# Block sums of the gated tokens on VectorE instead of GpSimd, next tokens' steps at every second unit, and the last product by output half

## The chip, the cores and the metric

The kernel runs on one core of a Trainium2 chip. The metric is the time of one execution on the device, in microseconds (us).

## The reference

Three layers follow each other: attention with keys and values averaged in groups of 8, a layer of products `(a * b @ w3) @ w_out`, and a layer with a gate. The change touches the last alone:

```python
def _moe2_ref(x, w_in, w_out):        # x: 4608 x 512, w_in: 512 x 2048, w_out: 2048 x 512
    h = x @ w_in
    g = h * (1.0 / (1.0 + np.exp(-1.702 * h)))
    return (g @ w_out).astype(np.float32)
```

## The kernel before

Tokens are taken in 9 blocks of 512. Every factor of a product is kept as two parts, a rounded one ("hi", made by a cast on ScalarE) and its residue ("lo", a subtraction on VectorE); each product is three matmuls of 128x512 (`mm3u`, L709). The last layer handles block 0 plainly and the other eight in four passes of two blocks (`for pr`, L911), in which each pair of 2x2 block products is done with seven products instead of eight (M1 to M7), as in Strassen's scheme: the factors are sums and differences of blocks.

A pass has two parts. The **gate part** runs over four groups `fp` of the hidden dimension. In each, PE does the products of `ORDER` (84 matmuls, and in the first three groups 12 more, "O", for the output); ScalarE and VectorE bring them from PSUM into the tiles g11, g12, g22 and g21 and apply the gate (`gelu`, L858). At the end of a group three block sums are formed (L987, GpSimd): g11 = g12 - g11, t2 = g22 - g11 and g12 = g22 - g12. They are factors of the output products.

The **output part** (from L1022) has six products (`OUT`: M2, M6, M5, M7, M4, M3) of four units each, 24 units of 12 matmuls; the first unit is followed by 12 more for M1. After each unit `make` prepares one more moving tile (`mv`, four buffers): a cast (L104) on ScalarE and a residue (L105) on VectorE from one of the block sums. Beside it each unit takes one step of `late` (the results of the product before: add L1017, transpose L730, four stores L736) or, where there is none, one of `prep`. `prep` is the twelve steps of `x_prep` for the next pass's tokens: the load of four tiles (L784, SP), eight differences (L792, each with a cast and a residue, tiles sx and xM), and three splits (L109, L110). A fourth block sum per group, g21 = g21 - t2 (L1004, GpSimd), follows four of the `make` steps.

Weights stream through six slots (`pull`, L702, tiles st) on SP's queue. In pass 1 there are also the 32 steps `wsum` on weights (L826, L831, L832, L834), a few of them in each group.

The order of instructions on each engine is not the code's order: a planner lays them out when the program is built, by their order in the code and by when it takes them to be ready. On the chip each engine runs its list in that order.

Of the kernel before, what the change touches and what calls it, by code (L numbers as in the profile page):

```python
# [12 lines left out]
ALU = mybir.AluOpType  # L13
# [4 lines left out]
P = 128  # L18
T = 512
# [3 lines left out]
def pooled_attention_moe_moe2(  # L23
# [648 lines left out]
    with tc.tile_pool(name="pb", bufs=1, reuse_waits="tile") as pb, \  # L672
# [7 lines left out]
        def freed(*bs):  # L680
            for i, _ in bs:
                banks.append(i)
# [43 lines left out]
        def out_tile():  # L726
            return pb.tile([P, T // 32, 2, 32], F32, name="ot", tag="ot")
# [129 lines left out]
        def gelu(o, i):  # L857
            nc.scalar.activation(o, i, AF.Gelu_apprx_sigmoid)  # L858
# [52 lines left out]
        for pr in range(1, NPAIR + 1):  # L911
            X = xc.pop(pr)
            bA = []
            G = []
            mvs = {}

            def out_mm(bs, name, fp, first, last):
                g, w = mvs.pop((name, fp)), ready.pop(("o", pr, name, fp))
                for m in range(2):
                    for i in range(2):  # L920
                        mm3u(bs[m][1], w[:, i], m, g[:, :, i], first and i == 0, last and i == 1)
                pull()

            for fp in range(NFP):
                g11, g12, g22, g21, t2 = (gtile(a * NFP + fp) for a in range(5))
                G.append((g11, g12, g22, g21, t2))
                C, Z, W = [None] * 2, [None] * 2, [None] * 2
                m1, U, V = [None] * 2, [None] * 2, [None] * 2
                for name, i in ORDER:
                    if name == "O":  # L930
                        if fp < NFP - 1:
                            if fp == 0:
                                bA += [bank() for _ in range(2)]
                            out_mm(bA, "M1", fp, fp == 0, False)
                        continue
                    if name in PART:
                        s, h = PART[name]
                        w = ready[s, pr, 2 * fp + i][:, h]
                    else:
                        w = ready[name, pr, fp][:, i]  # L940
                    bs = W if name == "M2" else Z if name in ("M5", "M3") else C
                    first = name in ("M1", "M2", "M5")
                    if first:
                        bs[i] = bank()
                    o = bs[i][1]
                    for j in range(2):
                        mm3u(o, w, j, X[name][:, :, j], first and j == 0, j == 1)
                    if name == "M1":
                        m1[i] = tmp("m")
                        nc.scalar.copy(m1[i], o)  # L950
                    elif name == "M2":
                        ready.pop(("a", pr, 2 * fp + i))
                        pull()
                        nc.vector.tensor_tensor(out=g11[:, i], in0=o, in1=m1[i], op=ALU.add)
                        freed(W[i])
                        if i:
                            gelu(g11, g11)
                            g = mvs["M1", fp] = moving()
                            split(g, g11, nc.vector)
                    elif name == "M6":  # L960
                        U[i] = tmp("u")
                        nc.scalar.copy(U[i], o)  # L962
                    elif name == "M5":
                        ready.pop(("s", pr, 2 * fp + i))
                        pull()
                    elif name == "M7":
                        V[i] = tmp("m")
                        nc.scalar.copy(V[i], o)
                        nc.vector.tensor_tensor(out=g22[:, i], in0=Z[i][1], in1=V[i], op=ALU.add)
                        if i:  # L970
                            gelu(g22, g22)
                    elif name == "M4":
                        gelu(g21[:, i], o)
                        freed(C[i])
                    elif name == "M3":
                        nc.vector.tensor_tensor(out=g12[:, i], in0=o, in1=U[i], op=ALU.add)
                        freed(Z[i])
                        if i:
                            gelu(g12, g12)
                    if i and name in ("M7", "M4", "M3"):  # L980
                        ready.pop((name, pr, fp))
                        pull()
                    if wsum and (name, i) in (("M2", 1), ("M5", 0), ("M7", 0), ("M4", 0),
                                              ("M6", 1), ("M7", 1), ("M4", 1)):
                        wsum.pop(0)()
                for o, p, m in ((g11, g12, g11), (t2, g22, g11), (g12, g22, g12)):
                    nc.gpsimd.tensor_tensor(out=o, in0=p, in1=m, op=ALU.subtract)  # L987
            while wsum:
                wsum.pop(0)()


            prep = x_prep(pr + 1) if pr < NPAIR else []
            src = {"M5": 0, "M7": 1, "M3": 2, "M2": 3, "M4": 3, "M6": 4}
            todo_mv = [(name, fp) for name, _ in OUT for fp in range(NFP)]
            t4 = list(range(NFP))

            def make():
                if todo_mv:
                    name, fp = todo_mv.pop(0)
                    g = mvs[name, fp] = moving()  # L1000
                    split(g, G[fp][src[name]], nc.vector)
                    if t4 and (name, fp) in (("M6", 0), ("M6", 2), ("M5", 0), ("M5", 2)):
                        t = G[t4.pop(0)]
                        nc.gpsimd.tensor_tensor(out=t[3], in0=t[3], in1=t[4], op=ALU.subtract)  # L1004

            m1, U, V, n = [], [], [], 0
            b0, b1 = 2 * pr - 1, 2 * pr
            late = []

            def out_of(name, bs):  # L1010
                ot = out_tile()
                add, blk, i = {"M2": (m1, b0, 0), "M7": (V, b1, 1),
                               "M4": (None, b0, 1), "M3": (U, b1, 0)}[name]

                def part(m):
                    if add:
                        nc.vector.tensor_tensor(out=add[m], in0=bs[m][1], in1=add[m], op=ALU.add)  # L1017
                    turn_out(ot, m, add[m] if add else bs[m][1])

                def end():  # L1020
                    part(1)
                    store(ot, blk, i)  # L1022

                return [lambda: part(0), end]

            make()
            make()
            for name, u in OUT:
                if name == "M2":
                    bW = [bank() for _ in range(2)]  # L1030
                elif name == "M5":
                    bZ = [bank() for _ in range(2)]
                bs = bW if name == "M2" else bZ if name in ("M5", "M3") else bA
                for fp in range(NFP):
                    out_mm(bs, name, fp, name in ("M2", "M5") and fp == 0, fp == NFP - 1)
                    make()
                    if name == "M2" and fp == 0:
                        out_mm(bA, "M1", NFP - 1, False, True)
                        for m in range(2):
                            m1.append(tmp("m"))  # L1040
                            nc.scalar.copy(m1[m], bA[m][1])
                        make()
                    if late:
                        late.pop(0)()
                    elif prep:
                        prep.pop(0)()
                    n += 1
                if name == "M6":
                    for m in range(2):
                        U.append(tmp("u"))  # L1050
                        nc.scalar.copy(U[m], bA[m][1])
                elif name == "M7":
                    for m in range(2):
                        V.append(tmp("m"))
                        nc.scalar.copy(V[m], bA[m][1])
                if name in ("M2", "M7", "M4", "M3"):
                    late += out_of(name, bZ if name == "M7" else bs)
                if name == "M2":
                    freed(*bW)
                elif name == "M4":  # L1060
                    freed(*bA)
            while late:
                late.pop(0)()
            freed(*bZ)
            while prep:
                prep.pop(0)()

# [29 lines left out]
```

## Time and profile before

| | us |
|---|---|
| three runs | 1496.11, 1495.22, 1498.04 (median 1496.11) |
| the profiled run | 1496.16 |
| span of the profiled run, first to last instruction | 1494.0 |
| busy in that span: PE | 1441.0 |
| VectorE (DVE) | 962.9 |
| ScalarE (ACT) | 693.8 |
| GpSimd (POOL) | 662.1 |

The four passes run from 856 us to the end. Times in the rows below are microseconds from the span's start, durations in microseconds unless marked ns. PE is the matmuls, SPq and ACTq are the queues that issue transfers. A row of a timeline may hold several instructions of one kind, with their count; in brackets stands how long the engine was idle before it and what ended that. Matmuls are pipelined: one has a record of 0.39 us, and the next begins before it ends.

### The profile page before, as it was taken

To read this page: it belongs to the slowest core of one execution; us is meant where nothing else is said; L and a number is where in the kernel's file an instruction comes from. 1 tells how busy PE (TensorE), PEld (TensorE's weight loads), DVE (VectorE), ACT (ScalarE), POOL (GpSimd) and SP (SyncE) were. 2 spreads that over 40 slices of the span, in tenths; PEclk is the share of its full clock that TensorE was granted. 3 is DMA by queue.
4 is the path that set the end of the run, shared out by engine and by line. 5 is a ranking of instruction groups with operands and counts; after the bars stand their busy time and mean duration, and the time that the engine had idled before them with its cause. 6 is when DMAs were issued, how large, how long until landed. Compare 5 with 4: busy or idle time off the path is not lost.

```text
span 1494.0 us, 19448 instructions
## 1 busy us (share of the span) xinstructions
PE 1441.0 (96%) x6536; PEld 1189.5 (80%) x6536; DVE 962.9 (64%) x1664; ACT 693.8 (46%) x1212; POOL 662.1 (44%) x653
## 2 busy tenths in 40 slices
PE   4988999999999999999999998999999999999998
PEld 3766888888888888888888876778877888788886
DVE  7888998878787877555627255583339433853354
ACT  6974444434343433365635344442455244534442
POOL 7787856555555555366833122500532043302530
PEclk9989999999999999999999999999999999999999
DMA  9991342323232311199879887767676866786665
GB/s 276 242 226 34 65 89 52 77 49 77 48 77 48 76 33 37 61 321 350 307 248 385 285 271 269 272 184 230 198 231 214 230 195 213 230 235 187 200 208 138
DMA packets 292323, 267.64 MB, mean 179 GB/s; under 512 B 199552, under 2 KB 224128, under 8 KB 292224
## 3 DMA queue, kind: packets, MB, share of 16 engines
q1 hardware_dynamic: 291648, 265.35, 59.0%
q10 hardware_dynamic: 576, 1.05, 0.2%
q8 instruction: 52, 0.85, 0.2%
q14 instruction: 47, 0.39, 0.1%
HBM read 209.72 MB, written 56.62 MB: 178 GB/s over the span
## 4 chain that ended last, share of the span: by engine, by line
PE 83%; DVE 6%; DMA 5%; ACT 2%; issue 2%; POOL 2%; SPq 0%; DVEq 0%; POOLq 0%; ACTq 0%
PE bk L709 38%; PE wk L114 8%; PE wk L116 8%; PE wk L115 8%; PE acc L114 5%; PE acc L116 4%; PE acc L115 4%; PE wk L278 2%; DMA xM<-x2d 2%; PE bk L115 1%; PE bk L116 1%; PE bk L114 1%; POOL cv L172 1%; DVE p L314 1%; DMA st<-wud 1%
## 5 line engine op out<-in xcount | busy, mean ns | idle before, releaser
L709 PE MATMUL bk<-mv,st 128*128 128x512 f32 x1104 | 263.6, 394 | 9.6 <-DVE mv L105 4.6
L709 PE MATMUL bk<-xM,st 128*128 128x512 f32 x1140 | 268.4, 390 | 1.9 <-ACT u L962 1.9
L709 PEld LDWEIGHTS bk<-mv,st 128*128 128x128 f32 x1104 | 209.2, 190 | 56.3 <-DVE mv L105 5.9
L709 PEld LDWEIGHTS bk<-xM,st 128*128 128x128 f32 x1140 | 214.4, 188 | 46.9 <-ACT u L962 2.3
L114 PE MATMUL wk<-s,s 128*128 128x512 f32 x576 | 228.1, 398 | 6.5 <-DVE a L641 3.8
L987 POOL TENSOR_TENSOR s<-g,s 128x1024 f32<-128x1024 f32 x16 | 38.8, 2423 | 426.0 <-ACT g L858 426.0
L115 PE MATMUL wk<-s,s 128*128 128x512 f32 x576 | 225.5, 392 | 0.1
L116 PE MATMUL wk<-s,s 128*128 128x512 f32 x576 | 225.3, 392 | 0.1
L314 DVE STREAM_TRANSPOSE p<-s_t 32x160 f32<-32x160 f32 (+1 forms) x560 | 178.5, 319 | 10.5
L105 POOL TENSOR_TENSOR s<-a,s 128x512 fp32r<-128x512 f32 x56 | 73.4, 1310 | 155.0 <-ACT s L104 121.2
L116 PE MATMUL acc<-s,s 128*128 128x512 f32 x352 | 139.4, 396 | 1.8 <-DVE s L105 1.8
L105 DVE TENSOR_TENSOR mv<-g,mv 128x1024 fp32r<-128x1024 f32 x80 | 112.9, 1411 | 43.8 <-ACT mv L104 42.6
L115 PE MATMUL acc<-s,s 128*128 128x512 f32 x352 | 139.5, 396 | 1.2 <-POOL s L105 1.1
L114 PE MATMUL acc<-s,s 128*128 128x512 f32 x352 | 131.9, 400 | 7.6 <-DVE s L105 4.5
L114 PEld LDWEIGHTS wk<-s,s 128*128 128x128 f32 x576 | 108.9, 189 | 30.8 <-DVE a L641 5.0
L116 PEld LDWEIGHTS wk<-s,s 128*128 128x128 f32 x576 | 108.7, 189 | 23.3 <-DVE s L105 0.5
L115 PEld LDWEIGHTS wk<-s,s 128*128 128x128 f32 x576 | 108.6, 189 | 22.2 <-DVE s L391 0.5
L172 POOL TENSOR_TENSOR cv<-cv,s 128x512 int32<-128x512 int32 x72 | 100.8, 1409 | 34.1 <-DVE cv L169 22.4
L104 ACT CAST mv<-g 128x1024 fp32r<-128x1024 f32 x80 | 84.1, 1053 | 64.9 <-PE bk L709 62.3
L114 PEld LDWEIGHTS acc<-s,s 128*128 128x128 f32 x352 | 66.7, 190 | 22.2 <-ACT s L104 5.0
L116 PEld LDWEIGHTS acc<-s,s 128*128 128x128 f32 x352 | 66.8, 190 | 15.6 <-DVE s L105 3.0
L115 PEld LDWEIGHTS acc<-s,s 128*128 128x128 f32 x352 | 66.8, 190 | 14.5 <-POOL s L105 2.3
(188 smaller groups left out, 2469.6 us busy)
## 6 DMA issues: line engine op xcount, KB each, us to landing
st<-wud SPq DMA_DIRECT2D x92, 512.0 KB, 4.2
st<-wind SPq DMA_DIRECT2D x66, 512.0 KB, 4.7
st<-wind SPq DMA_DIRECT2D x84, 256.0 KB, 4.0
s<-in_moe_w_dram SPq DMA_DIRECT2D x32, 512.0 KB, 6.2
wind<-s SPq DMA_DIRECT2D x32, 512.0 KB, 5.2
s<-in_moe_w_out_dram SPq DMA_DIRECT2D x24, 512.0 KB, 6.8
s<-wud SPq DMA_DIRECT2D x20, 512.0 KB, 4.5
kr<-in_k_dram SPq DMA_DIRECT2D x128, 72.0 KB, 2.5
```

The costliest lines, as they stand in the source:

```text
L104: nc.scalar.copy(dst[:, 0], src)
L105: lo_eng.tensor_tensor(out=dst[:, 1], in0=src, in1=f32(dst[:, 0]), op=ALU.subtract)
L114: nc.tensor.matmul(o, a[:, 0, a_sl], b[:, 0, b_sl], start=first, stop=False)
L115: nc.tensor.matmul(o, a[:, 0, a_sl], b[:, 1, b_sl], start=False, stop=False)
L116: nc.tensor.matmul(o, a[:, 1, a_sl], b[:, 0, b_sl], start=False, stop=last)
L172: nc.gpsimd.tensor_tensor(out=w.bitcast(I32), in0=w.bitcast(I32), in1=lo_w.bitcast(I32), op=ALU.add)
L278: nc.tensor.matmul(sc[half][:, i * KW:(i + 1) * KW], qT[:, sl(tt)], mov, start=True, stop=True)
L314: nc.vector.transpose(out=dst[:, :nt, 32 * c:32 * c + 32], in_=s_t[32 * c:32 * c + 32, :nt, 32 * r:32 * r + 32])
L709: nc.tensor.matmul(o, w[:, x, m], b[:, y], start=first and n == 0, stop=last and n == 2, skip_group_check=True)
L987: nc.gpsimd.tensor_tensor(out=o, in0=p, in1=m, op=ALU.subtract)
```

## The change

The block sums move from GpSimd to VectorE. The three of a group are put on a list `tsum` and issued one by one in the next group, behind M2's second half, M6's first and M5's first; those of the last group are issued in the first units of the output part. The fourth sum of each group goes onto the same list, two to four units later in the code than before (behind M6's third moving tile, M5's first and third, and M7's first). In the output part a unit without a step of `late` now issues one sum, if the list holds one, and the steps `prep` come at every second unit whether there is a step of `late` or not. In the last pass the last product, M3, is done for output half 0 over all groups and then for half 1; each half is added, transposed and stored by itself, with the four stores on the queues of SP and ACT in turn, and all remaining moving tiles are made ahead of the product.

```diff
-            G = []
+            G, tsum = [], []
             mvs = {}
+
+            def t_sub():
+                if tsum:
+                    o, p, m = tsum.pop(0)
+                    nc.vector.tensor_tensor(out=o, in0=p, in1=m, op=ALU.subtract)
...
+                    if (name, i) in (("M2", 1), ("M6", 0), ("M5", 0)):
+                        t_sub()
                     if i and name in ("M7", "M4", "M3"):
...
-                for o, p, m in ((g11, g12, g11), (t2, g22, g11), (g12, g22, g12)):
-                    nc.gpsimd.tensor_tensor(out=o, in0=p, in1=m, op=ALU.subtract)
+                tsum += [(g11, g12, g11), (t2, g22, g11), (g12, g22, g12)]
...
-                    if t4 and (name, fp) in (("M6", 0), ("M6", 2), ("M5", 0), ("M5", 2)):
+                    if t4 and (name, fp) in (("M6", 2), ("M5", 0), ("M5", 2), ("M7", 0)):
                         t = G[t4.pop(0)]
-                        nc.gpsimd.tensor_tensor(out=t[3], in0=t[3], in1=t[4], op=ALU.subtract)
+                        tsum.append((t[3], t[3], t[4]))
...
+                if pr == NPAIR and name == "M3":
+                    while late:
+                        late.pop(0)()
+                    while todo_mv:
+                        make()
+                    ot = out_tile()
+                    gw = [(mvs.pop((name, fp)), ready.pop(("o", pr, name, fp)))
+                          for fp in range(NFP)]
+                    for m in range(2):
+                        for fp, (g, w) in enumerate(gw):
+                            for i in range(2):
+                                mm3u(bs[m][1], w[:, i], m, g[:, :, i], False,
+                                     fp == NFP - 1 and i == 1)
+                        nc.vector.tensor_tensor(out=U[m], in0=bs[m][1], in1=U[m], op=ALU.add)
+                        turn_out(ot, m, U[m])
+                        rows = out[b1 * T:(b1 + 1) * T]
+                        for b in range(4):
+                            (nc.scalar if b % 2 else nc.sync).dma_start(
+                                rows[:, b * P + m * 32:b * P + m * 32 + 32].rearrange(
+                                    "(c t) o -> t c o", t=32),
+                                ot[32 * b:32 * b + 32, :, m])
+                    freed(*bZ)
+                    break
...
+                    n += 1
                     if late:
                         late.pop(0)()
-                    elif prep:
+                    elif tsum:
+                        t_sub()
+                    if prep and n % 2:
                         prep.pop(0)()
-                    n += 1
```

## Rows read from the trace of the kernel before

**Rows 1.** Head of the page: span and instructions.
```profile
span 1494.0 us, 19448 instructions
```
**Rows 2.** Stretches: bounds, length, busy us and instructions by engine, clock, transfers.
```profile
core 0: us, PE busy (x) PEld busy (x) DVE busy (x) ACT busy (x) POOL busy (x), PEclk, DMA share, GB/s
...
1102.00:1172.00 70.00, 67.60 (x296) 55.47 (x297) 55.38 (x55) 36.20 (x45) 13.14 (x5) 1.00 0.71 225
...
1330.00:1410.00 80.00, 80.00 (x355) 66.26 (x354) 26.51 (x30) 31.90 (x44) 25.76 (x10) 1.00 0.66 199
```
**Rows 3.** Waits of PE from 856 us on: total us, times, longest.
```profile
PE bk L709 <- DVE mv L105: 4.6, 4, 3.9
PE bk L709 <- ACT mv L104: 4.1, 3, 1.6
PE bk L709 <- ACT u L962: 2.7, 2, 1.9
PE bk L709 <- DMA st<-wud: 2.2, 2, 1.4
PE bk L709 <- DMA s<-wud: 1.1, 1, 1.1
```
**Rows 4.** Timeline of PE, passes 1 and 2: start, us, instruction, [idle before].
```profile
920.28 4.63 PE L709 MATMUL bk<-mv,st 128*128 128x512 f32 x10 [3.89 <-DVE mv L105]
...
1133.46 0.50 PE L709 MATMUL bk<-mv,st 128*128 128x512 f32 x1 [1.28 <-ACT mv L104]
1134.19 7.75 PE L709 MATMUL bk<-mv,st 128*128 128x512 f32 x33 [0.23 <-DVE mv L105]
```
**Rows 5.** Stretches behind two pauses of PE in pass 1.
```profile
920.30:925.50 5.20, 5.20 (x12) 4.11 (x13) 1.73 (x3) 1.06 (x1) 0.00 (x0) 0.50 0.94 331
...
976.60:980.30 3.70, 3.70 (x9) 2.89 (x10) 3.70 (x5) 0.95 (x3) 0.00 (x0) 0.54 0.40 84
```
**Rows 6.** Timeline of DVE, output part of pass 2.
```profile
1122.77 1.70 DVE L792 TENSOR_TENSOR sx<-xM,sx 128x512 f32<-128x512 f32 x1 [1.12 <-DMA xM<-x2d]
1124.39 3.42 DVE L105 TENSOR_TENSOR mv<-g,mv 128x1024 fp32r<-128x1024 f32 x1
```
**Rows 7.** Line 105 from 856 us on: duration ns min/median/max, first and last start.
```profile
L105 DVE TENSOR_TENSOR mv<-g,mv x80: 1198/1226/3434, 879.6 to 1478.1; 128x1024 fp32r<-128x1024 f32 x80
...
L105 DVE TENSOR_TENSOR xM<-sx,xM x24: 674/685/2879, 957.5 to 1310.1; 128x512 fp32r<-128x512 f32 x24
```
**Rows 8.** Timeline of POOL, the same stretch of pass 2.
```profile
1123.88 2.85 POOL L987 TENSOR_TENSOR g<-g,g 128x1024 f32<-128x1024 f32 x1
```
**Rows 9.** Timeline of ACT, the same stretch.
```profile
1131.85 0.62 ACT L104 CAST xM<-sx 128x512 fp32r<-128x512 f32 x1 [5.52 <-DVE sx L792]
```
**Rows 10.** Timeline of DVE, gate part of pass 1.
```profile
911.45 1.81 DVE L832 TENSOR_TENSOR wt<-ws,wt 128x512 fp32r<-128x512 f32 x1 [3.64 <-ACT wt L831]
913.29 5.00 DVE L826 TENSOR_TENSOR ws<-wq 128x256 f32<-128x256 f32 x2
918.22 0.41 DVE L826 TENSOR_TENSOR ws<-ws,wq 128x256 f32<-128x256 f32 x1
...
919.01 1.22 DVE L105 TENSOR_TENSOR mv<-s,mv 128x1024 fp32r<-128x1024 f32 x1
```
**Rows 11.** Timeline of POOL, the same stretch of pass 1.
```profile
907.85 2.39 POOL L987 TENSOR_TENSOR s<-g,s 128x1024 f32<-128x1024 f32 x1 [19.56 <-ACT g L858]
```
**Rows 12.** The chain that ended last, its last row.
```profile
1488.60 0.71 DVE ot L730
```
**Rows 13.** Timeline of SP's queue, the last stores.
```profile
1489.34 1.96 SPq L736 DMA_DIRECT2D out_dram<-ot  x4
```
**Rows 14.** Transfers by line: count, KB each, median us from issue to landing.
```profile
kr<-in_k_dram SPq DMA_DIRECT2D x128, 72.0 KB, 2.5
...
out_dram<-ot SPq DMA_DIRECT2D x72, 128.0 KB, 3.2
```
**Rows 15.** Timeline of PE in the gate part of pass 3.
```profile
1190.74 0.62 PE L709 MATMUL bk<-mv,st 128*128 128x512 f32 x2
...
1192.55 1.98 PE L709 MATMUL bk<-mv,st 128*128 128x512 f32 x8
...
1195.73 0.62 PE L709 MATMUL bk<-mv,st 128*128 128x512 f32 x2
```

More of the change, by code (lines that the diff above doesn't have):

```diff
@@ L1061, in pooled_attention_moe_moe2 @@
                     freed(*bA)
-            while late:
-                late.pop(0)()
-            freed(*bZ)
+            else:
+                while late:
+                    late.pop(0)()
+                freed(*bZ)
             while prep:
```

## The prediction

> **What bounds the kernel now.** I began with the span, 1494.0 us [rows 1] for a profiled run of 1496.16, so 2.16 us lie outside the records; the median of the runs, 1496.11, is the same number for this purpose. Everything in the diff lies in the four pair passes, the last 630 us. The table by stretches shows what bounds them: in a stretch without a pause PE is busy all of 80.00 us with 355 matmuls [rows 2], 80.00/355 = 0.225 us each, at the full granted clock. So PE is the bound there, and no other engine's work counts unless PE waits for it. What can be won is PE's pauses, and the table of waits from 856 us on lists them all [rows 3]: 4.6 + 4.1 + 2.7 + 2.2 + 1.1 = 14.7 us of idle time in 12 pieces. Next I asked where they lie, in PE's timeline, and what they cost beyond the idle time.
>
> The longest is in pass 1: 3.89 us before 920.28, for DVE's residue of a moving tile [rows 4]. After it the granted clock is 0.50, the lower level, and 12 matmuls take 5.20 us [rows 5]; 12 x 0.225 = 2.7, so 2.5 us more. Together 6.4. Three alike lie in the output products of passes 1, 2 and 3 (one stands in rows 4; the others are at 975.84 and 1288.93): PE waits for a cast on ACT, does one matmul, and waits for DVE's residue. The waits on ACT are 4.1 together, those on DVE 4.6 - 3.9 = 0.7 [rows 3]. The one matmul between takes 1134.19 - 1133.46 = 0.73 instead of 0.225, of which 0.23 is counted already, so 0.27 more in each, 0.8. After the one in pass 1 the clock is 0.54 for 3.70 us with 9 matmuls [rows 5], which should take 2.0: 1.7 more. Together 4.1 + 0.7 + 0.8 + 1.7 = 7.3. The other pieces, 2.7 on the copy u and 3.3 on weight transfers, are 6.0.
>
> Then I asked why DVE was late. In pass 2 a residue takes 3.42 us and the step before it 1.70 [rows 6], where the median residue of that shape is 1.226; a half-size residue (the next instruction) reaches 2.879 against a median of 0.685 [rows 7]. GpSimd is in its block sums just then, back to back [rows 8]: DVE's 1124.39 instruction spans GpSimd's 1123.88 one and ends 1.1 us behind it. An instruction that reads two SBUF operands waits here while GpSimd runs one. ACT is dragged along: its cast xM waits 5.52 us for DVE's step, with the moving tiles' casts queued behind [rows 9]. In pass 1 it is the same: two 128x256 instructions take 5.00 us where the next like it takes 0.41, and the residue that PE wants starts only at 919.01 [rows 10].
>
> **The change part by part.** It removes GpSimd's 16 sums in each pass (2.39 and 2.85 us in the two rows shown [rows 8, 11]), and with them all GpSimd work in the four passes. It adds as many to DVE. No plain f32 difference of 128x1024 on DVE stands in the trace; the nearest row is the residue of the same size and operands, minimum 1.198 and median 1.226 [rows 7]. I take 1.23, with 1.20 and 1.30 as bounds: 64 x 1.23 = 79 us over four passes.
>
> Off the path these cost nothing while DVE has room. In the gate part DVE is busy 26.51 of 80.00 us [rows 2], and three sums per group of 21.6 us (96 matmuls) add 3.7, so about half. In the output part DVE is busy 55.38 of 70.00 [rows 2], some 6 of it waiting for GpSimd (below); with seven sums, 7 x 1.23 = 8.6, that is 58 of 70. The cover is thinner there, but the moving tiles have four buffers, so a residue may be about three units (3 x 12 x 0.225 = 8 us) early, less 2.3 for cast and residue.
>
> *Pass 1, 6.4 us.* DVE is idle until 911.45, then does a residue (1.81), the two long ones, two short ones and at 919.01 the wanted residue [rows 10]. Without GpSimd: 911.45 + 0.69 + 4 x 0.42 = 913.8, and the residue would end at 915.1, ahead of PE, which is out of work at 916.4. The three sums of the previous group can start when GpSimd starts them now, at 907.85 [rows 11], 3.6 us before 911.45, and DVE idles for just that long [rows 10]; three sums of 1.23 fit if the order puts them there. If all queue behind 911.45, the residue ends at 915.1 + 3.7 = 918.8, and the wait is only 1.5 us shorter. I take 5.4 us of gain, nearer the idle slot; bounds 1.5 and 6.4.
>
> *Output parts of passes 1 to 3, 7.3 us.* In pass 2's stretch the blocked time goes: (3.42 - 1.23) + (2.88 - 0.69) + (1.70 - 0.69) = 5.4 us. Three sums of the last group and the first of the gated tokens come: 4.9 us. Balance only -0.5. But the same edit also moves the next tokens' steps to every second unit, so at least one difference with its residue (2 x 0.69 = 1.4 us on DVE, and its cast on ACT) leaves this stretch, and the fourth block sum is asked for two units later. That is 0.5 + 1.4 + 1.2 = 3.1 us less in front of a residue that was 1.8 us late. I keep 0.2 each, a gain of 6.7; bounds 1.5 (the balance alone, three times) and 7.3. The load of the next tokens, four transfers on SP, stays at the first unit, so nothing on SP is moved past anything else; its landing still sits in front of the first difference. Of the last steps, the one for M1, which the next pass wants first, moves to unit 18 of 0 to 23, five units (13.5 us) ahead of it; the one for M3, at unit 22, is wanted only at the end of the next pass's first group.
>
> *The weight transfer of 1.1 us in pass 1* [rows 3] was issued behind a store that waited for a blocked DVE residue. I take 0.5, bounds 0 and 1.1. The other 4.9 us (u copies, weight slots) I leave as they are. Whether a new order makes them larger or smaller the trace can't say; bounds -3 and +3 us.
>
> *The last product.* Today the chain ends PE, add, transpose, add, transpose at 1489.3 [rows 12], then four stores issued in 1.96 us on SP [rows 13]; the span ends 2.7 us behind the last issue. Output half 0 will be done 24 matmuls (5.4 us) early, its add, transpose and four stores under the other half. Half 1's add still waits for the last matmul, so DVE ends where it did; then two stores on each of two queues: two issue slots of 0.5 us saved, 1.0 us. The stores move half the bytes in runs of 128 instead of 256 bytes. The nearest rows are 128-KB stores in 256-byte runs, 3.2 us to landing, and 72-KB loads in 128-byte runs, 2.5 [rows 14], so I price a half store at no more than a whole one. Bounds 0 and 1.1. All moving tiles of this product are made ahead of it, so the fourth is wanted after 18 matmuls (4.1 us) rather than 36; cast and residue need 2.3 after the buffer comes free, so no new wait. The single output tile must be rid of M4's stores by the first transpose: two transposes, 1.96 us of issues and 2 to 3 of landing put that about 6 us after M4's end, and the transpose comes 6.1 after it (5.4 + 0.7). A microsecond of wait there would lie under the other half's matmuls.
>
> Against the last product stands a rule of the Trainium skill (DMA: Bandwidth & Descriptors, Specifications): transfers under 512 bytes are not at line rate, since the engine then reads, modifies and writes. Both kinds of run are under that here, and no row shows a store of 128-byte runs. If by it a half store took as long as a whole one and the two queues shared the engines, the tail would give about 0.5 instead of 1.0 (an estimate), and the time would be 1483.1.
>
> Sum: 5.4 + 6.7 + 0.5 + 1.0 = 13.6. 1496.16 - 13.6 = **1482.6**, DVE's added 79 us off the path.
>
> **The rivals.** *DVE takes GpSimd's place.* The sums stand where the blocking stood, and nothing is deferred: gains 1.5 + 1.5 + 1.0 = 4.0, so 1492.2, from 1489 to 1496. For it: DVE at 58 of 70 us, and its waits for the next tokens' landing, which block all behind them. Against: the four-buffer lead.
>
> *Transfers are late next.* A PE that runs sooner asks for weights sooner. In passes 2 and 3 it already waits 2.2 us for them [rows 3]. One more wait of 1.5 us in each of three passes: 1482.6 + 4.5 = 1487.1.
>
> *The spread doesn't take place.* The instructions' order on each engine is a planner's, not the code's: the 12 matmuls of one early output product run as 2, 8 and 2 among others [rows 15]. It may pull the next tokens' steps forward again, since DVE looks free to it. Then only the removal of GpSimd counts in the output parts, about half of the 6.7: 1486.
>
> *Slower: a sum in front of an add that empties PSUM.* In the gate part PE reuses banks that DVE's adds free; a 1.23 us sum started just before holds the add up, and ACT's gelu and copies behind it. If each of 16 groups paid one sum, 16 x 1.23 = 19.7 us would turn 1482.6 into 1502. It ends slower from 1.05 us per group ((13.6 + 3.0)/16). Against it: DVE is busy a third of that part and PE shows not one pause there in passes 2 to 4 away from the last group.
>
> **How the numbers follow.** Forecast 0.58 (own range 1478 to 1487). DVE in GpSimd's place 0.15, transfers 0.10, no spread 0.06, slower 0.07, and 0.04 that some of the other 4.9 us go as well (about 1477). A measurement of this kernel can tell about 0.2%, 3.0 us, from no change; so faster means under 1493.1. All of the forecast, transfers, no spread and better lie there (0.78), and 0.06 of the first rival: 0.84. The rest of it is "same", 0.09; slower 0.07. The range runs from 1477 to 1492: it takes in all but the upper half of the first rival, the slower one and a little below.
>
> **What would show it.** GpSimd without an instruction in the four passes; DVE residues all near 1.23 and 0.69, none above 1.5; no wait at 916 to 920 nor at the eighth output unit, and the clock at its full level behind them; the last store issued about 1 us earlier. I am wrong if PE's table of waits shows DVE as large as before, if a sum stands between a PE result and its add, or if waits for weights have grown by what was won.

## The result and the profile after

The changed kernel takes 1481.38 us (median of four runs, 1480.04 to 1482.07) against 1495.99 (1495.22 to 1498.04): 14.6 us less, a ratio of 0.9891 with a 95% interval of 0.9871 to 0.9910. The forecast was 1482.6. The profiled run is the one of 1480.04 us, and its span is 15.7 us shorter, so that the trace shows about 1.1 us more gain than the medians.

The page's head and the row of its part 1 (busy us, share of the span, instructions of each engine):

```profile
span 1478.3 us, 19409 instructions
...
PE 1437.1 (97%) x6536; PEld 1188.0 (80%) x6536; DVE 991.5 (67%) x1728; ACT 696.6 (47%) x1212; POOL 491.9 (33%) x589
```

Against [rows 1] that is 1494.0 - 1478.3 = 15.7 us less. GpSimd has 64 instructions fewer and is idle throughout the four passes; its 491.9 us all lie ahead of them.

The waits of PE from 856 us on, total us, times, longest, as in [rows 3]:

```profile
PE bk L709 <- ACT u L967: 2.2, 2, 1.7
PE bk L709 <- DMA st<-wind: 1.3, 2, 0.7
PE bk L709 <- DMA st<-wud: 0.5, 1, 0.5
PE bk L709 <- DMA s<-wind: 0.5, 1, 0.5
```

14.7 us in 12 pieces have become 4.5 in 6. DVE and the moving tiles' casts, 8.7 us of the 14.7, are gone from the list. Counted from the start of one matmul to the start of the next, pauses and slow clock together, PE lost 21.9 us in the passes before and loses 7.0 now; with 0.7 us at the tail that is the span's 15.7 to within 0.1.

Why DVE no longer holds PE up is seen in the table of line 105, DVE's residues (duration ns min/median/max), the counterpart of [rows 7], and in a row of the new line 920, the block sums:

```profile
L105 DVE TENSOR_TENSOR mv<-g,mv x80: 1215/1224/1228, 880.8 to 1463.1; 128x1024 fp32r<-128x1024 f32 x80
...
L105 DVE TENSOR_TENSOR xM<-sx,xM x24: 681/685/694, 951.5 to 1294.9; 128x512 fp32r<-128x512 f32 x24
```

```profile
L920 DVE TENSOR_TENSOR g<-g,g x32: 1218/1220/1223, 879.6 to 1416.8; 128x1024 f32<-128x1024 f32 x32
```

The longest residue fell from 3434 ns to 1228, the longest half-size one from 2879 to 694; the medians stayed. A sum takes 1.22 us on DVE.

By stretches (columns as in [rows 2]): the changed kernel is 12 us ahead when pass 2's output part begins, and 16 us in pass 4, so stretches of equal work are set side by side. First the output part of pass 2 in the kernel before and in the changed one, 330 matmuls each; then the piece of the gate part of pass 4 that [rows 2] shows, in the changed kernel:

```profile
1103.20:1179.80 76.60, 75.09 (x330) 61.65 (x329) 55.65 (x57) 35.34 (x43) 11.94 (x5) 1.00 0.73 227
...
1091.00:1165.60 74.60, 74.60 (x330) 61.76 (x330) 53.58 (x61) 35.75 (x43) 0.00 (x0) 1.00 0.75 233
...
1314.00:1395.10 81.10, 80.52 (x354) 66.11 (x353) 36.97 (x42) 32.12 (x44) 0.00 (x0) 1.00 0.66 200
```

PE has no pause in the output part now, where it was busy 75.09 of 76.60 us before. DVE is busy for less time (53.58 against 55.65), though it runs four instructions more. In the gate part DVE went from 26.51 to 36.97 us, and PE, which had no pause there, is busy 80.52 of 81.10: that pause is the weights' (DMA st<-wind).

### The profile page after: what moved, and what is told of

It reads as the page before. It is cut to its first block, busy times and chain, and to the rows that moved or that the text cites. A ratio compares the mean times of both kernels' runs of the same rounds, so it can differ in the third digit from the quotient of the medians.

```text
span 1478.3 us, 19409 instructions
## 1 busy us (share of the span) xinstructions
PE 1437.1 (97%) x6536; PEld 1188.0 (80%) x6536; DVE 991.5 (67%) x1728; ACT 696.6 (47%) x1212; POOL 491.9 (33%) x589
## 4 chain that ended last, share of the span: by engine, by line
PE 82%; DVE 7%; DMA 5%; ACT 2%; POOL 2%; issue 1%; SPq 1%; DVEq 0%; ACTq 0%; POOLq 0%
PE bk L709 39%; PE wk L114 8%; PE wk L116 8%; PE wk L115 8%; PE acc L114 4%; PE acc L115 4%; PE acc L116 4%; PE wk L278 2%; DMA wud<-wt 2%; DVE s L105 1%; DVE cv L169 1%; PE bk L114 1%; PE bk L115 1%; PE bk L116 1%; POOL cv L172 1%
## 5 line engine op out<-in xcount | busy, mean ns | idle before, releaser
L709 PE MATMUL bk<-mv,st 128*128 128x512 f32 x1104 | 258.7, 389 | 0.5 <-DMA st<-wud 0.5
L115 PE MATMUL acc<-s,s 128*128 128x512 f32 x352 | 141.2, 401 | 1.0 <-POOL s L105 0.8
L116 PE MATMUL acc<-s,s 128*128 128x512 f32 x352 | 140.7, 400 | 1.6 <-DVE s L105 1.6
L114 PE MATMUL acc<-s,s 128*128 128x512 f32 x352 | 134.1, 406 | 8.1 <-DVE s L105 5.4
L105 DVE TENSOR_TENSOR mv<-g,mv 128x1024 fp32r<-128x1024 f32 x80 | 97.8, 1222 | 32.5 <-ACT mv L104 31.0
L104 ACT CAST mv<-g 128x1024 fp32r<-128x1024 f32 x80 | 84.5, 1056 | 71.3 <-PE bk L709 70.8
L114 PEld LDWEIGHTS acc<-s,s 128*128 128x128 f32 x352 | 67.9, 194 | 23.3 <-ACT s L104 4.7
L116 PEld LDWEIGHTS acc<-s,s 128*128 128x128 f32 x352 | 67.9, 193 | 15.8 <-DVE s L105 2.7
L115 PEld LDWEIGHTS acc<-s,s 128*128 128x128 f32 x352 | 68.0, 193 | 14.4 <-POOL s L105 2.0
L638 ACT COPY a<-wk 128x512 f32<-128x512 f32 x72 | 42.1, 585 | 68.3 <-PE wk L116 68.1
```

The costliest lines, as they stand in the source:

```text
L104: nc.scalar.copy(dst[:, 0], src)
L105: lo_eng.tensor_tensor(out=dst[:, 1], in0=src, in1=f32(dst[:, 0]), op=ALU.subtract)
L114: nc.tensor.matmul(o, a[:, 0, a_sl], b[:, 0, b_sl], start=first, stop=False)
L115: nc.tensor.matmul(o, a[:, 0, a_sl], b[:, 1, b_sl], start=False, stop=False)
L116: nc.tensor.matmul(o, a[:, 1, a_sl], b[:, 0, b_sl], start=False, stop=last)
L638: nc.scalar.copy(a, pa_)
```

## The experiments

Theory A is the prediction's: PE paused because DVE instructions with two SBUF operands stood still while GpSimd ran a sum. Its rivals say that the spread of the next tokens' steps did it, that GpSimd's sums were slow to deliver, or that DVE was short of time. In `gp_reads`, `gp_writes`, `dve_1_more` and `dve_2_more` instructions are added whose result isn't used; the other kernels only undo or move parts of the change, or go one step on.

### One part at a time

`sums_alone` is the changed kernel without the spread and without the last product by half:

```diff
-                if pr == NPAIR and name == "M3":
...
                     n += 1
+                    if tsum and not late:
+                        t_sub()
                     if late:
                         late.pop(0)()
-                    elif tsum:
-                        t_sub()
-                    if prep and n % 2:
+                    elif prep:
                         prep.pop(0)()
```

> The kernel before with the 64 block sums on DVE alone: the next tokens' steps stay at every unit, the last product stays as it was. Theory A (blocking: the pauses of PE came from DVE instructions standing still while GpSimd ran a sum): everything but the tail's gain is here, 1481.4 + 0.7 = 1482.1 us, DVE's residues all near 1.22 us. Rival B (the spread carries half of the gain in the output parts, as one of the prediction's rivals has it): about 1485 us, with pauses of 1 us or more left in the output parts of passes 1 to 3.

Measured: 1483.68 us where the kernel before, on the same chip, took 1498.13; ratio 0.9909 (0.9889 to 0.9928), 14.5 us less. The time alone lies between the two forecasts, 1482.1 and about 1485. The trace decides for theory A: no residue of DVE is among PE's waits, and there is no pause in the output parts. Of the list's four rows two are transfers of weights, 2.1 us together, and the others are

```profile
PE bk L709 <- ACT u L967: 2.8, 2, 1.9
...
PE bk L709 <- DVE g L974: 1.0, 1, 1.0
```

`spread_alone` is the kernel before with this alone:

```diff
+                    n += 1
                     if late:
                         late.pop(0)()
-                    elif prep:
+                    if prep and n % 2:
                         prep.pop(0)()
-                    n += 1
```

> The kernel before with the next tokens' steps at every second unit and nothing else: the sums stay on GpSimd. Theory A (blocking): the residues still reach 3.4 us and the pause at 916 to 920 us stays; of the 7.3 us in the output parts at most half goes, 1492 to 1496 us. Rival B (the spread is what cures the output parts): these three pauses vanish, 1488.7 us. Rival C (the planner puts the steps where it did before): 1496 us, no change.

Measured: 1496.78 us, ratio 0.9999 (0.9980 to 1.0018), no change. Residues still reach 3422 ns, and PE's largest waits are those of before:

```profile
PE bk L709 <- ACT mv L104: 5.2, 3, 2.4
PE bk L709 <- DVE mv L105: 3.8, 3, 3.4
```

It is rival C that holds: in the four passes DVE's 356 instructions, ACT's 356 and SP's 378 transfers stand in the same order as in the kernel before (compared by the tiles' names and the shapes).

`last_alone` is the kernel before with the block `if pr == NPAIR and name == "M3"` of the change alone.

> The kernel before with the last product by output half and nothing else. The tail from PE's last matmul to the end of the span should shrink from 6.2 to 5.5 us, as it did in the changed kernel: 1495.3 us, 0.7 less. If the 1.0 us of the prediction is the right size, 1495.0. If a run of 128 bytes makes a store slower, as much as before or more, 1496 us.

Measured: 1496.65 us, ratio 0.9991 (0.9978 to 1.0003), too small to tell from none. The trace does show a gain: from PE's last matmul to the span's end 5.5 us, 6.2 before.

`no_spread` takes the spread alone back out of the changed kernel (the second hunk of `sums_alone`), beside an unchanged copy, `after_again`.

> The changed kernel once more, unchanged, so that the two beside it have it on the same chip. 15 us below the kernel before (ratio 0.990); its passes from the first product on some 619.4 us, DVE not among PE's releasers.

> The changed kernel with the next tokens' steps back at every unit that has no step of the last results; sums on DVE and the last product by half stay. Theory A (blocking alone): as the changed kernel, within 1 us. If the spread is worth what the sums alone seemed to lack (their passes took 622.2 us against 619.4): 2 to 3 us more than the changed kernel beside it, with a pause of PE on an add of DVE in the gate part of pass 2.

Measured beside each other: 1482.97 us (ratio 0.9907, 0.9885 to 0.9929) with the edit for the spread, 1482.20 (0.9902, 0.9882 to 0.9922) without. This does not price a spread, because none takes place: DVE's 420 instructions of the passes, ACT's 356 and SP's 378 transfers have the same order with the edit and without it, and `sums_alone` has that order too, up to the last stores. The two kernels here are repeats of one order, and the 0.8 us between their medians is noise.

The unchanged copy's profiled run had a span of 1484.4 us, 6.1 more than the first one's, and its passes took 623.5 us, not 619.4, so two parts of the expectation failed: 619.4 was too sharp, and PE's list does name DVE (an add, L974, twice, 1.8 us; who ended these two pauses is taken up under the prediction below). PE's pauses are 6.8 us together instead of 4.5, most of the difference at places where weights land, and the mean granted clock from 856 to 946 us is 0.98 instead of 1.00. One execution differs from the next by that much, so the 2.8 us that the sums alone seemed to lack need no cause.

So all of the gain that the times can tell is the sums' move; the 0.7 us at the tail show in traces alone. Is it DVE's freedom from GpSimd, or the sums' earlier results? The trace of the kernel before speaks against the second: in the passes one instruction waited for a sum of GpSimd (`ACT mv L104 <- POOL s L987: 1.9, 1, 1.9`), and PE never did.

### GpSimd put back beside the sums

`gp_reads` leaves every sum on DVE and adds idle GpSimd work that reads what the sum wrote:

```diff
+        scr = pb.tile([P, 2, 448], mybir.dt.bfloat16, name="scr", tag="scr")
...
                     nc.vector.tensor_tensor(out=o, in0=p, in1=m, op=ALU.subtract)
+                    nc.gpsimd.tensor_tensor(
+                        out=scr, in0=o[:, :, :448], in1=o[:, :, 64:], op=ALU.subtract)
```

> The changed kernel, and behind each of its 64 sums on DVE an idle GpSimd difference of 128x896 elements that reads the sum's result from SBUF into a small tile that nothing uses; DVE's order stays what it was. Theory A (blocking): DVE instructions with two SBUF operands stand still again, residues up to 2 to 3.4 us, and pauses of PE on DVE or ACT come back: 6 to 14 us of the 14.6 won are lost, 1487 to 1495 us. Rival E (GpSimd's sums were simply slow to deliver their results, 2.4 us each in a row, and the products waited for these): nothing waits for the new instructions, so 1481.4 us and residues at 1.22.

Measured: 1520.99 us, ratio 1.0162 (1.0147 to 1.0177): not 6 to 14 but 40 us lost, so that it is slower than the kernel before. The direction is theory A's and excludes the rival: no engine's wait names GpSimd, and DVE and ACT run the changed kernel's instructions in the same order. The size I had taken from the residues. The sums themselves read two SBUF operands, and here they stand in DVE's list and are held up too. Line 105 and the sums (now line 921), then DVE and POOL in the output part of pass 2, and PE's waits:

```profile
L105 DVE TENSOR_TENSOR mv<-g,mv x80: 1204/1222/3154, 884.3 to 1504.7; 128x1024 fp32r<-128x1024 f32 x80
```

```profile
L921 DVE TENSOR_TENSOR g<-g,g x32: 1209/2548/3156, 881.2 to 1457.6; 128x1024 f32<-128x1024 f32 x32
```

```profile
1136.72 3.13 DVE L921 TENSOR_TENSOR g<-g,g 128x1024 f32<-128x1024 f32 x1
1139.78 3.09 DVE L105 TENSOR_TENSOR mv<-g,mv 128x1024 fp32r<-128x1024 f32 x1
1142.79 0.68 DVE L1026 TENSOR_TENSOR m<-bk,m 128x512 f32<-128x512 f32 x1
```

```profile
1133.27 14.07 POOL L922 TENSOR_TENSOR scr<-g 128x896 bf16<-128x896 f32 x5 [1.23 <-DVE g L921]
```

```profile
PE bk L709 <- DVE mv L105: 21.7, 8, 6.5
```

Through five GpSimd instructions in a row, a sum and a residue take 3.1 us each. The add between them (L1026) takes its first operand from PSUM, and 0.68 us as ever. PE waits 21.7 us for DVE; all its pauses are 30.3 us, against 4.5 in the changed kernel, and the mean granted clock of the span fell from 0.994 to 0.984.

`gp_writes` has GpSimd read one column and then only write:

```diff
+        scr = pb.tile([P, 448], F32, name="scr", tag="scr")
+        nc.gpsimd.memset(scr, 0.0)
...
+                    nc.gpsimd.tensor_copy(scr[:, :1], o[:, 0, :1])
+                    for _ in range(4):
+                        nc.gpsimd.memset(scr, 0.0)
```

> As the one before, but GpSimd reads a single column of the sum and then fills the small tile four times with a constant, which reads nothing from SBUF. If it is GpSimd's reading that holds DVE up: residues near 1.22 us, no new pauses, 1481 to 1482.5 us. If any work of GpSimd on SBUF holds DVE up: residues lengthened by as much as a fill takes, and some microseconds of pauses, from 1484 us up.

Measured: 1484.04 us, ratio 0.9909 (0.9889 to 0.9929), the changed kernel's own within the interval. The median stands at the lower end of the second forecast (from 1484 us up), so the time does not decide; the trace does. GpSimd's fills keep it busy for 121.1 us in the passes (count, busy us, mean ns), the residues don't notice, and neither they nor the casts are among PE's waits:

```profile
L925 POOL MEMSET scr<- 128x448 f32 x256 | 121.1, 473 | 14.8
```

```profile
L105 DVE TENSOR_TENSOR mv<-g,mv x80: 1216/1224/1227, 883.3 to 1467.6; 128x1024 fp32r<-128x1024 f32 x80
```

So it is GpSimd's reading of SBUF that holds up a DVE instruction with two SBUF operands, not its being busy, nor its writing. The Trainium skill says so (SBUF — State Buffer, Who interferes with whom): a DVE instruction with two SBUF inputs contends with a GpSimd instruction that reads SBUF, not with one that only writes it. Both halves agree with these two runs, 3154 against 1227 ns at the longest.

### How much room DVE has

`dve_1_more` and `dve_2_more` add two and four DVE instructions behind each sum (below the first; the second has `range(4)`):

```diff
+        scr = pb.tile([P, 448], F32, name="scr", tag="scr")
+        nc.vector.memset(scr, 0.0)
...
+                    for j in range(2):
+                        nc.vector.tensor_tensor(
+                            out=scr, in0=o[:, j % 2, :448], in1=scr, op=ALU.subtract)
```

> The changed kernel, and behind each of the 64 sums two more differences of 128x448 on DVE into a tile that nothing uses, some 1.2 us together: 79 us more on DVE, as much again as the change added. If DVE has the room that the prediction counts on (39 of 86 us busy in the gate part, 52 of 70 in the output part): no more than 2 us, up to 1483.5 us. If DVE is at its edge already (rival: DVE in GpSimd's place): a pause of about 1 us for most groups, 1490 us or more.

> Four such differences behind each sum: 158 us more on DVE, about 69 of 86 us busy in the gate part. If the room ends somewhere here, PE's pauses come back with DVE or ACT named as the releaser: 1484 to 1495 us. If nothing happens even so, 1483 us or less, DVE's share of busy time has no bearing in this stage, only the length of a single wait has.

Measured: 1482.36 us (ratio 0.9903, 0.9889 to 0.9918) and 1483.31 (0.9915, 0.9893 to 0.9936). With 79 us more on DVE nothing happens. With 158 more the time is between the two forecasts, and no difference stands clear of the interval, but a first wait of 1.1 us on a residue appears, and one of 1.0 us that the list puts down to an add. The planner lays DVE's and ACT's lists anew for both kernels, so they tell what more work on DVE costs here, not what it costs in the changed kernel's order. In `dve_2_more` the gate and the output part of pass 2 read (columns as before):

```profile
1003.90:1090.50 86.60, 85.75 (x377) 70.40 (x376) 62.29 (x87) 34.09 (x46) 0.00 (x0) 1.00 0.70 216
1090.70:1167.00 76.30, 75.16 (x330) 61.62 (x330) 69.91 (x93) 36.36 (x44) 0.00 (x0) 1.00 0.68 218
```

DVE is busy 69.91 of 76.30 us there, and the 1.1 us are PE's only pause. So the rival "DVE takes GpSimd's place" was not near: with 158 us on DVE beyond the 79 of the change, one residue comes late in this part.

### The sums at once, and a step further

`at_once` issues the sums in the code where the kernel before had them, on DVE:

```diff
                 tsum += [(g11, g12, g11), (t2, g22, g11), (g12, g22, g12)]
+                for _ in range(3):
+                    t_sub()
...
-                    if t4 and (name, fp) in (("M6", 2), ("M5", 0), ("M5", 2), ("M7", 0)):
+                    if t4 and (name, fp) in (("M6", 0), ("M6", 2), ("M5", 0), ("M5", 2)):
                         t = G[t4.pop(0)]
                         tsum.append((t[3], t[3], t[4]))
+                        t_sub()
```

> The changed kernel with the sums on DVE traced at once at the end of each group, and the fourth behind the same moving tiles as before, instead of one by one from a list. Theory A with the planner setting the order by readiness: the same pauses, 1480.5 to 1483 us. Rival D (the spreading in the code keeps a sum from standing in front of an add that PE waits for): pauses of PE on ACT or DVE at the head of each group, from 0.3 to 1.2 us in 16 groups, 1486 to 1500 us.

Measured: 1483.15 us, ratio 0.9904 (0.9883 to 0.9926), as the changed kernel. The traces say why: DVE's, ACT's and SP's instructions of the passes stand in the changed kernel's order. The planner's order makes the list superfluous.

`wt_two` goes after what is left in pass 1. From the fourth of the eight steps `f` on, the second pair of casts goes to another tile, 5 of the 16 casts:

```diff
-                t = pb.tile([P, 2, 2, HU], F32R, name="wt", tag="ot")
+                t = pb.tile([P, 2, 2, HU], F32R, name="wt",
+                            tag="g19" if n and f >= 3 else "ot")
```

> The changed kernel, and in pass 1 every second pair of converted weight sums goes to a tile that is free until the last group, instead of sharing the one tile ot. What is left of PE's pauses in pass 1, 2.5 us on the copy u behind a cast that waits for a store out of that tile, should go in part: 1 to 2.5 us below the changed kernel beside it. If these pauses come from something else (the next tokens' landing, weights): no difference.

Measured: 1479.27 us, ratio 0.9886 (0.9865 to 0.9906), 3.7 below the changed kernel beside it, more than the 1 to 2.5 expected. The two intervals overlap, so the time alone doesn't settle whether it is faster. The profile shows that the pause went: the wait on u is gone from PE's list, which has 2.5 us left, and PE is busy throughout the stretch where it stood.

```profile
900.00:960.00 60.00, 60.00 (x266) 49.71 (x265) 37.86 (x49) 33.92 (x47) 0.00 (x0) 1.00 0.85 297
```

By the medians it is the fastest of all.

## Why the prediction was right, point by point

**What bounds the kernel** held: PE's pauses were all there was to win, and the span shrank by what they shrank. The sum, 5.4 + 6.7 + 0.5 + 1.0 = 13.6, reads in the traces 6.4 + 7.3 + 1.5 + 0.7 = 15.9, to the span's 15.7: both blocked stretches gave all they had, the other pauses went from 6.0 to 4.5 us, the tail gave less. That 1482.6 came within 1.2 us of the median is partly luck: six runs of the unchanged copy lie between 1477.61 and 1486.10, and the second term was right in size for a reason that did not hold (below).

**GpSimd's blocking** held, and is shown: `sums_alone` has 14.5 of the 14.6 us, and `gp_reads` brings pauses back with the order of DVE and ACT unchanged. The price of a sum on DVE, 1.23 us from a residue's row, measured 1.22.

**Pass 1**, 6.4 us, of which I had expected to win 5.4: the pause before 920.28 [rows 4] and its half clock [rows 5] are gone. DVE does the sums where I put them, in its idle time. The timeline of DVE there, against [rows 10] (gaps marked):

```profile
907.66 1.22 DVE L920 TENSOR_TENSOR s<-g,s 128x1024 f32<-128x1024 f32 x1
...
909.39 1.22 DVE L920 TENSOR_TENSOR g<-g,s 128x1024 f32<-128x1024 f32 x1
910.52 2.36 DVE L920 TENSOR_TENSOR g<-g,g 128x1024 f32<-128x1024 f32 x2
912.79 1.22 DVE L105 TENSOR_TENSOR mv<-s,mv 128x1024 fp32r<-128x1024 f32 x1
```

The residue that began at 919.01 begins at 912.79. The blocking is not the whole of these 6.2 us: the planner now has the residue ahead of the five steps on weights (L832 and four of L826) that stood in front of it, which I had not foreseen. The blocking alone is enough for a pause, though. `gp_reads` has the new order, and PE waits 2.48 us there for this residue:

```profile
921.84 3.10 DVE L105 TENSOR_TENSOR mv<-s,mv 128x1024 fp32r<-128x1024 f32 x1
```

In the changed kernel a pause of 2.2 us stays in nearly the same place all the same, by a cause that I had put among the 4.9 us left as they are: PE's timeline has

```profile
912.57 0.70 PE L709 MATMUL bk<-mv,st 128*128 128x512 f32 x2 [0.49 <-DMA st<-wud]
914.97 1.65 PE L709 MATMUL bk<-xM,s 128*128 128x512 f32 x6 [1.69 <-ACT u L967]
```

and ACT's names what the copy u stood behind:

```profile
913.81 0.62 ACT L831 CAST wt<-ws 128x512 fp32r<-128x512 f32 x1 [2.15 <-DMA wud<-wt]
914.33 0.58 ACT L967 COPY u<-bk 128x512 f32<-128x512 f32 x1
```

A cast waits for the store out of the one tile it writes, and everything on ACT waits with it. `wt_two` gave 5 of the 16 casts another tile, and the pause went.

**Output parts**, 7.3 us, of which I had expected to win 6.7: all gone. The size was right and the step behind it wrong. I let the balance of blocked time against added sums be only 0.5 us and had the later steps and the later fourth sum take 2.6 us (1.4 + 1.2) out of the stretch. The edits to the code did neither: without the spread (`no_spread`) and with the fourth sum at its old place in the code (`at_once`) DVE's order is the same, and the fourth sum is in this stretch, at 1112.64. The changed kernel (sums and ends of the stretch, gaps marked), then three of the four residues in the kernel before (the other is in [rows 6]):

```profile
1104.92 1.22 DVE L105 TENSOR_TENSOR mv<-g,mv 128x1024 fp32r<-128x1024 f32 x1 [0.63 <-ACT mv L104]
1106.07 1.22 DVE L920 TENSOR_TENSOR s<-g,s 128x1024 f32<-128x1024 f32 x1
...
1108.34 1.22 DVE L920 TENSOR_TENSOR g<-g,s 128x1024 f32<-128x1024 f32 x1
1109.47 1.22 DVE L920 TENSOR_TENSOR g<-g,g 128x1024 f32<-128x1024 f32 x1
1112.03 0.69 DVE L792 TENSOR_TENSOR sx<-xM,sx 128x512 f32<-128x512 f32 x1 [1.34 <-DMA xM<-x2d]
1112.64 1.22 DVE L920 TENSOR_TENSOR g<-g,g 128x1024 f32<-128x1024 f32 x1
...
1116.71 1.22 DVE L105 TENSOR_TENSOR mv<-g,mv 128x1024 fp32r<-128x1024 f32 x1
```

```profile
1117.09 1.23 DVE L105 TENSOR_TENSOR mv<-g,mv 128x1024 fp32r<-128x1024 f32 x1 [0.63 <-ACT mv L104]
1119.31 2.34 DVE L105 TENSOR_TENSOR mv<-g,mv 128x1024 fp32r<-128x1024 f32 x1 [1.00 <-ACT mv L104]
...
1132.94 1.20 DVE L105 TENSOR_TENSOR mv<-g,mv 128x1024 fp32r<-128x1024 f32 x1
```

From the first residue to the end of the fourth DVE takes 1117.93 - 1104.92 = 13.0 us; the same four took 1134.14 - 1117.09 = 17.1 before. The stretch has four sums more in it and is 4.0 us shorter, where 1.8 were needed. What made up for the 2.6: a second blocked residue (2.34 us at 1119.31), left out of my sum, was 1.1; one transpose and one step, which the planner puts behind the fourth residue once the sums are on DVE, 1.4; and the sums lie partly in gaps in which DVE waited for ACT and for the next tokens' landing. That landing still holds DVE up (1.34 us), as said, and costs PE nothing.

**The spread doesn't take place** was a rival, at 1486 us. Its condition came true, and its price was wrong: it let the removal of GpSimd alone win about half of the output parts' 6.7 us, and that won all of it.

**Seven sums in the output part** was wrong too: four. The fourth sums of the first three groups stood in the gate part before the change already; I had read their place from the code, not from GpSimd's timeline. That step bore on the cover alone, and with four sums it was thicker than I had reckoned.

**The weight transfer of 1.1 us** in pass 1 is gone in this run (0.5 forecast). Waits of 0.5 to 0.7 us on other weights have come in the gate parts, 1.8 us of idle time, not the 4.5 of the rival "transfers are late next"; and with those that went, PE's waits for weights fell from 3.3 to 2.3 us together.

**The last product** gave 0.7 instead of 1.0. The last row of the chain and the stores as issued, against [rows 12, 13], and the stores by line (KB each, median us to landing), against [rows 14]:

```profile
1473.58 0.71 DVE ot L730
```

```profile
1471.37 3.79 SPq L1057 DMA_DIRECT2D out_dram<-ot  x4
1471.37 3.87 ACTq L1057 DMA_DIRECT2D out_dram<-ot  x4
```

```profile
out_dram<-ot SPq DMA_DIRECT2D x4, 64.0 KB, 2.1
out_dram<-ot ACTq DMA_DIRECT2D x4, 64.0 KB, 2.3
```

Half 0's stores begin at 1471.37, and its add began 3.0 us ahead of half 1's rather than 5.4, so the planner took up matmuls of half 1 before half 0 was done. That cost nothing, since only half 1's stores end the kernel. Their issuing gave what I took: the last issue ends 0.95 us behind the last transpose (1475.24 - 1474.29), 2.0 before. What is missing lies behind it: the span ends 3.1 us after the last issue, here and in `last_alone`, and 2.7 before. Why is open. Stores of 64 KB in runs of 128 bytes land in 2.1 to 2.3 us; the last four of 128 KB in the kernel before took 2.4 (median), so half the bytes come hardly sooner. At the tail, 0.7 lies between the 1.0 that I took and the 0.5 that I estimated from the Trainium skill's rule on transfers under 512 bytes (DMA: Bandwidth & Descriptors, Specifications). No run has a store of 64 KB in longer runs, so none shows what the rule costs here.

**Slower by a sum ahead of an add**: no such wait. PE's list does name an add of DVE in some traces, for about 1 us: once in `sums_alone` and `wt_two`, twice in the unchanged copy `after_again`. But the add is not what PE waited for. One of these places in the changed kernel's first trace and in `after_again`, which is the same program:

```profile
1069.39 1.62 PE L709 MATMUL bk<-xM,s 128*128 128x512 f32 x6
1069.56 0.69 DVE L974 TENSOR_TENSOR g<-bk,m 128x512 f32<-128x512 f32 x1 [1.54 <-ACT m L973]
```

```profile
1073.55 0.69 DVE L974 TENSOR_TENSOR g<-bk,m 128x512 f32<-128x512 f32 x1 [1.54 <-ACT m L973]
1074.27 1.63 PE L709 MATMUL bk<-xM,s 128*128 128x512 f32 x6 [0.93 <-DVE g L974]
```

In the first trace the matmul begins before the add does, so it cannot need it. In both it begins 0.13 us behind the landing of a weight tile (at 1069.26 and 1074.14), and at the other four places, that of `dve_2_more` among them, a weight tile lands 0.14 us before. These pauses are put down to the weights. (The threshold in that rival, (13.6 + 3.0)/16, is 1.04 us, not 1.05.)

## What to carry to other kernels

Where PE's list of waits names DVE, look at the longest of DVE's instructions, not at its busy share or its mean: a median of 1.23 us with a maximum of 3.4, as here, can mean that something else holds it up. Off the path, a GpSimd instruction that reads SBUF can cost more than the same work on a DVE that is 90% busy. Where a planner sets each engine's order, read an instruction's place from the trace before pricing an edit that moves it in the code, and compare the orders of two kernels before reading their times as a test: `spread_alone`, `no_spread` and `at_once` had the very order of the kernel that they were set against.

## What the runs showed of the hardware that I had not expected

That GpSimd's fills leave DVE alone: 256 of them, 121 us, and no residue above 1227 ns, while 64 reading differences of the same engine cost 40 us. And the blocking goes both ways: GpSimd's copy of one column takes 0.18 us when it is alone, but 1.05 when it starts under a DVE residue that began at 1111.26 and ended at 1112.48 (both from `gp_writes`):

```profile
1111.26 1.22 DVE L105 TENSOR_TENSOR mv<-g,mv 128x1024 fp32r<-128x1024 f32 x1
...
1111.48 1.05 POOL L923 COPY scr<-s 128x1 f32<-128x1 f32 x1 [16.77 <-DVE s L922]
...
1114.72 0.18 POOL L923 COPY scr<-g 128x1 f32<-128x1 f32 x1
```
